# Issuing nine raw parts of w_in from the sync queue, behind the keys and score blocks of chunk 0

## The chip, the cores and the metric

The kernel runs on one core of a Trainium2 chip. The metric is the device time of one execution in microseconds (us). Before the change it is 875.8 us, the median of three runs (874.41 to 876.63). The profiled execution has a span of 874.3 us.

## The reference: delta-rule attention, then a two-layer feed-forward block

There are 4 batches of 8 heads, a sequence of 768 positions and a head size of 48. The attention block keeps a 48 x 48 state per head and walks through the sequence:

```python
k_n = k / (norm(k) + 1e-6)
for t in range(768):
    y[t]  = q[t] @ state
    state = state + beta[t] * outer(k_n[t], v[t] - k_n[t] @ state)
```

Its output, 3072 tokens of 384 numbers, goes through

```python
h = x @ w_in                          # w_in: 384 x 2048
out = (h * sigmoid(1.702 * h)) @ w_out   # w_out: 2048 x 384
```

Both weights reach the kernel as 64-bit floating point, because a 32-bit array is multiplied by a 64-bit scalar where they are made. The kernel has to turn them into 32-bit numbers by itself.

## The kernel before

The sequence is cut into 6 chunks of 128 positions. A unit is one chunk of one batch, so there are 24 units. For every unit the kernel loads keys (KN), queries (QP) and values (V), normalizes the keys, forms score blocks G (keys with keys, keys with queries), writes the key scores to DRAM (Nd) and reads their diagonal 32 x 32 blocks back in another layout (NT). From these, VectorE works out the inverses of triangular blocks (`invert`), and TensorE then solves the units block by block. The feed-forward matmuls (`ph`, `po`) are mixed in between the attention steps as soon as their inputs exist.

For chunk 0 the keys of all four batches are loaded first, and the order is:

```python
    for i in range(B):
        for t, src, dma in ((KN, k, nc.sync.dma_start), (QP, q, nc.scalar.dma_start)):
            if i < len(t):                      # 4 KN tiles, 3 QP tiles at the start
                nc.vector.memset(t[i][:, :, D:DP], 0.0)
                load(i, ((t, src),), dma)
    ...                                         # beta (bI) on the scalar queue
    # -- cut --
    sync = pinned(nc.sync.dma_start)
    for b in range(0, B, HB):
        normalize_first(b)                      # b = 0,1 and then b = 2,3 on VectorE
    ahead(1)                                    # first raw parts of w_in
    run(weights(1, None))                       # convert part 0
    first = [prepare(b) for b in range(B)]
    for b in range(B + 1):
        if b < B:
            next(first[b])                      # transposes of the keys of b
            next(first[b])                      # ... and of the queries
            if b == 0:
                load(len(QP), ((QP, q),), pinned(nc.scalar.dma_start))
            warm(NA0)
        if b > 0:
            run(first[b - 1])                   # scores G of b - 1, then Nd and NT
    run(weights(W0 - 1, None))                  # convert parts 1 and 2
    for b in range(B):
        load_values(b, sync)
    ...
    for i in range(B, len(KN)):
        load(i, ((KN, k), (QP, q)), sync)       # keys and queries of units 4 to 6
    ahead(2)                                    # the next raw parts
    run(invert(0))
    normalize_first(B, len(KN) - B)
    run(weights(W1))
```

`pinned` keeps an instruction behind everything that the program has placed on its engine before. A DMA queue named "sync" is issued by the sync engine (SP in the profile, queue q1), "scalar" by ScalarE (ACT, q10), "gpsimd" by GpSimd (POOL, q0).

The raw weights are fetched in parts. The 12 parts of w_in (three row groups by four column blocks of 512) are staged in the space of w_out. There are six places for them, so parts 6, 7 and 8 take the places of parts 0, 1 and 2. Each fetch consists of four DMAs, for 48 + 16 + 48 + 16 partitions:

```python
    def stage(part):
        if part < parts_in:
            at = part % (2 * KC) * 2 * N_IN     # KC = 3: place part % 6
            return at, at + 2 * N_IN
        ...
    def fetch(part, dma):
        if part < parts_in:
            j, f0 = part % KC, part // KC * N_IN
            parts = list(range(part, part + (KC if part < 2 * KC else 1)))
            ...                                 # 3 parts at once for 0 and 3, else 1
    def convert(part):
        if part in stages:
            dst = target(part)
            from_double(dst, stages.pop(part), dst.shape[-1], part < NA)   # NA = 3
            made.append(part)
            while made and (len(made) > 1 or part >= n_parts - 8):
                taken.pop(made.pop(0), None)    # a place is given free one part later
    def ahead(n, dma=nc.gpsimd.dma_start):
        while n > 0 and waiting and free(waiting[0]):
            staged.extend(fetch(waiting.pop(0), dma))
            n -= 1
    def weights(n, dma=nc.gpsimd.dma_start):
        for _ in range(n):
            if staged:
                convert(staged.pop(staged.index(min(staged))))
            if dma is not None:
                ahead(2, dma)
            yield 0.0
```

`from_double` is six VectorE instructions on 128 x 512 elements for parts 0 to 2 (they are pinned), and five on VectorE and one on ScalarE for the later ones.

Of the kernel before, what the change touches and what calls it, by code (L numbers as in the profile page):

```python
# [18 lines left out]
def kernel(  # L19
# [28 lines left out]
    KC = DM // 128  # L48
# [10 lines left out]
    NA = W0  # L59
# [26 lines left out]
    def load(n, pairs, dma=nc.sync.dma_start):  # L86
        c, b = units[n]
        for dst, src in pairs:
            dma(
                out=dst[n % len(dst)][:, :, 0:D],  # L90
                in_=src[b, :, c * C : (c + 1) * C, :].rearrange("h p d -> p h d"),
            )
# [9 lines left out]
    def pinned(op):  # L102

        return lambda *a, **kw: tc.keep_in_program_order(op(*a, **kw))  # L104
# [45 lines left out]
    def from_double(dst, raw, n, alone):  # L150

        lo, hi = raw[:, :, 0], raw[:, :, 1]
        tmp = wk.tile([128, 2, n], I32, tag="P", name="tmp")
        t0, p = tmp[:, 0], tmp[:, 1]  # L160
        ts, stt = nc.vector.tensor_scalar, nc.vector.scalar_tensor_tensor
        if alone:
            ts, stt = pinned(ts), pinned(stt)
        AND, OR = ALU.bitwise_and, ALU.bitwise_or
        E1 = 1 << 20

        ts(p, hi, 0x7FF * E1, None, op0=AND)
        if alone:
            ts(p, p, -896.0 * E1, 0.0, op0=ALU.add, op1=ALU.max)
            ts(p, p, 255.0 * E1, 8.0, op0=ALU.min, op1=ALU.mult)  # L170
        else:
            nc.scalar.activation(p, p, ACT.Relu, scale=8.0, bias=low)
        ts(t0, hi, E1 - 1, E1, op0=AND, op1=OR)
        stt(out=dst, in0=lo.bitcast(U32), scalar=2.0**-32, in1=t0, op0=ALU.mult, op1=ALU.add)
        stt(out=p, in0=hi, scalar=-(1 << 31), in1=p, op0=AND, op1=OR)
        stt(out=dst, in0=dst, scalar=2.0**-20, in1=p.bitcast(F32), op0=ALU.mult, op1=ALU.mult)  # L176
# [3 lines left out]
    n_parts = parts_in + FC  # L180
# [12 lines left out]
    stages, taken, made = {}, {}, []  # L193

    def stage(part):

        if part < parts_in:
            at = part % (2 * KC) * 2 * N_IN
            return at, at + 2 * N_IN
        f = part - parts_in  # L200
        if f >= FC - 2:
            return None
        depth = 2 if f < 2 or f >= 8 else 4
        if f >= 12:
            depth = 1
        at = FC * DM // (2 if f < 2 else 1) - (f % depth + 1) * 2 * DM
        return at, at + 2 * DM

    def free(part):
        s = stage(part)  # L210
        return s is None or all(s[1] <= a or b <= s[0] for a, b in taken.values())

    def fetch(part, dma):

        if part < parts_in:
            j, f0 = part % KC, part // KC * N_IN
            parts = list(range(part, part + (KC if part < 2 * KC else 1)))
            shape, src = (len(parts), N_IN), moe_w_in[:, f0 : f0 + N_IN]
            dst = w_in[:, j : j + len(parts), f0 : f0 + N_IN]
        else:  # L220
            parts = [part]
            shape, src = (1, DM), moe_w_out
            dst = target(part)
        if src.dtype != F32:
            if (s := stage(part)) is None:
                raw = wk.tile([128, *shape, 2], I32, tag="xT", name="raw", bufs=3)
            else:
                words = slice(s[0], stage(parts[-1])[1])
                raw = w_out.rearrange("p f d -> p (f d)")[:, words].bitcast(I32)
                raw = raw.rearrange("p (j n o) -> p j n o", j=shape[0], o=2)  # L230
            for i, p in enumerate(parts):
                stages[p] = raw[:, i]
                if s is not None:
                    taken[p] = stage(p)
            dst = raw.bitcast(src.dtype).rearrange("p j n o -> p j (n o)")
        if part < parts_in:
            for p, r, m, step in x_rows:
                row = src[r + j * step : r + j * step + m]
                dma(
                    out=dst[p : p + m],  # L240
                    in_=bass.AP(
                        row.tensor, row.offset, [row.ap[0], [row.ap[0][0] * step, len(parts)], row.ap[1]]
                    ),
                )
        else:
            r = (part - parts_in) * 128
            dma(out=dst if src.dtype == F32 else dst[:, 0], in_=src[r : r + 128, :])
        return parts

    def target(part):  # L250
        if part < parts_in:
            j, f0 = part % KC, part // KC * N_IN
            return w_in[:, j, f0 : f0 + N_IN]
        return w_out[:, part - parts_in, :]
# [4 lines that stand above are left out]
            from_double(dst, stages.pop(part), dst.shape[-1], part < NA)  # L259

            made.append(part)
            while made and (len(made) > 1 or part >= n_parts - 8):
                taken.pop(made.pop(0), None)


# [19 lines left out]
    def normalize_first(b0, nb=HB):  # L285

        tt, ts = pinned(nc.vector.tensor_tensor), pinned(nc.vector.tensor_scalar)
        red, recip = pinned(nc.vector.tensor_reduce), pinned(nc.vector.reciprocal)
        stt = pinned(nc.vector.scalar_tensor_tensor)
        mult, add = ALU.mult, ALU.add  # L290
        z = wk.tile([128, 4, nb, H], F32, tag="ksq", name="z", bufs=1)
        sq = wk.tile([128, nb, H, D], F32, tag="G", name="sq", bufs=6)
        x, y, t, s = (z[:, i] for i in range(4))
        for b in range(nb):
            K = KN[(b0 + b) % len(KN)][:, :, 0:D]
            tt(sq[:, b], K, K, op=mult)
            red(s[:, b], sq[:, b], axis=AX.X, op=add)
        ts(x, s, 1e-30, None, op0=ALU.max)
        ts(y.bitcast(I32), x.bitcast(I32), -0.5, float(0x5F3759DF), op0=mult, op1=add)
        for _ in range(3):  # L300
            stt(out=t, in0=y, scalar=-0.5, in1=y, op0=mult, op1=mult)
            tt(t, t, x, op=mult)
            stt(out=y, in0=t, scalar=1.5, in1=y, op0=add, op1=mult)
        tt(s, s, y, op=mult)
        ts(s, s, 1e-6, None, op0=add)
        recip(s, s)
        for b in range(nb):
            K = KN[(b0 + b) % len(KN)][:, :, 0:D]
            tt(K, K, s[:, b].broadcast_to([128, H, D]), op=mult)
# [278 lines left out]
            nc.sync.dma_start(out=out[b * S + c * C : b * S + (c + 1) * C, :], in_=o)  # L588
            yield 1.3

    order = [0, KC] + list(range(2 * KC, n_parts))
    order[-3], order[-2] = order[-2], order[-3]
    waiting, staged = order[:], []

# [13 lines that stand above are left out]
# [11 lines left out]
    def run(work):  # L619
        for _ in work:  # L620
            pass
# [105 lines left out]
    sync = pinned(nc.sync.dma_start)  # L727
    for b in range(0, B, HB):
        normalize_first(b)
    ahead(1)  # L730
    run(weights(1, None))
    first = [prepare(b) for b in range(B)]
    for b in range(B + 1):
# [13 lines left out]
        nc.gpsimd.memset(KN[i][:, :, D:DP], 0.0)  # L747
    for i in range(B, len(KN)):
        load(i, ((KN, k), (QP, q)), sync)
    ahead(2)  # L750
    run(invert(0))
    normalize_first(B, len(KN) - B)
    run(weights(W1))
# [34 lines left out]
```

## Time and profile before

| | |
|---|---|
| Time, median of 3 | 875.8 us |
| Span of the profile | 874.3 us |
| TensorE matmuls busy | 805.2 us (92%) |
| VectorE busy | 488.7 us (56%) |
| ScalarE busy | 209.1 us (24%) |
| GpSimd busy | 115.9 us (13%) |
| DMA queue of the sync engine, q1 | 150528 packets, 40.78 MB |
| DMA queue of GpSimd, q0 | 3328 packets, 12.59 MB |
| DMA queue of ScalarE, q10 | 7168 packets, 1.41 MB |

The busy shares are means over stages that are very different. TensorE is nearly always busy after some 200 us; before that it waits for other engines and partly runs matmuls whose only use is to keep it active (`ps_warm`). In the answers of the trace, a line of the timeline gives the start, the duration, the engine, the line of the kernel, the operation and its tiles, and in brackets how long the engine was idle before it and what ended that. L104 stands for all pinned instructions, because their helper is on that line. The answers on DMA give packets, MB and the time that the packets took as a share of 16 engines; packets [...]overlap, so this share can pass 100%.

### The profile page before, as it was taken

What the parts mean: (1) busy time and instruction counts of PE and PEld (TensorE: products, weight loads), DVE (VectorE), ACT (ScalarE), POOL (GpSimd) and SP (SyncE); (2) the same over time, 40 slices, a digit from 0 to 9 for tenths busy, and PEclk for the clock granted to TensorE, in tenths of its full rate; (3) what the DMA queues carried; (4) which work ended last, traced back from release to release, by engine and by line L of the source; (5) the groups of instructions that cost most, each with busy time, mean ns of one, the idle gap of its engine ahead of it and who ended that gap; (6) DMA issues with size and microseconds to landing.
All of it is one profiled execution on the core that took longest, in us unless ns stands there. A gap on an engine that the chain in (4) does not pass through costs nothing.

```text
span 874.3 us, 15563 instructions
## 1 busy us (share of the span) xinstructions
PE 805.2 (92%) x6564; PEld 595.2 (68%) x6564; DVE 488.7 (56%) x1024; ACT 209.1 (24%) x407; POOL 115.9 (13%) x137
## 2 busy tenths in 40 slices
PE   7601988998999999999999999999999999999998
PEld 5401767865866866867867867867767768677684
DVE  3559968987985394493493592682672760110100
ACT  2300444352322221221312312312312202112020
POOL 3230331231021111101201102102100000000000
PEclk9655999999999999999999999999999999999999
DMA  9695582552223213213213223122132020000000
GB/s 145 118 186 66 124 227 55 137 123 67 47 61 81 49 34 81 49 42 73 57 39 67 59 52 73 38 62 60 25 72 55 3 48 9 1 23 1 14 10 18
DMA packets 161093, 55.76 MB, mean 64 GB/s; under 512 B 128800, under 2 KB 157696, under 8 KB 161024
## 3 DMA queue, kind: packets, MB, share of 16 engines
q1 hardware_dynamic: 150528, 40.78, 22.5%
q0 software_dynamic: 3328, 12.59, 6.3%
q10 hardware_dynamic: 7168, 1.41, 1.2%
q8 instruction: 51, 0.84, 0.4%
q14 instruction: 18, 0.15, 0.1%
HBM read 33.13 MB, written 20.45 MB: 61 GB/s over the span
## 4 chain that ended last, share of the span: by engine, by line
PE 82%; DVE 9%; DMA 6%; issue 1%; ACT 1%; POOL 1%; SPq 0%; DVEq 0%; POOLq 0%
PE po L580 28%; PE ph L565 27%; PE psG L337 5%; PE psY L503 5%; PE psR L478 5%; PE psU L490 4%; PE psT L323 2%; DMA KN<-in_k_dram 2%; PE psR L467 2%; DMA NT<-Nd 2%; PE ps_warm L138 2%; PE psS L522 2%; DVE P L104 1%; DMA Nd<-G 1%; DVE YB L104 1%
## 5 line engine op out<-in xcount | busy, mean ns | idle before, releaser
L565 PE MATMUL ph<-xT,w_in 128*128 128x256 f32 (+1 forms) x1248 | 269.3, 370 | 5.4 <-DMA xT<-last 3.2
L580 PE MATMUL po<-w_out,gT 128*128 128x384 f32 x768 | 268.1, 495 | 3.3 <-DVE w_out L176 3.3
L565 PEld LDWEIGHTS ph<-xT,w_in 128*128 128x128 f32 x1248 | 219.4, 192 | 42.8 <-issue 9.8
L580 PEld LDWEIGHTS po<-w_out,gT 128*128 128x128 f32 x768 | 140.5, 190 | 94.1 <-issue 9.0
L570 ACT ACTIVATE gT<-ph 128x512 f32<-128x512 f32 (+1 forms) x104 | 58.3, 564 | 184.0 <-PE ph L565 183.9
L486 DVE TENSOR_TENSOR V<-V,psR 32x384 f32<-32x384 f32 x92 | 50.6, 550 | 91.7 <-PE psR L478 85.3
L497 ACT COPY U<-psU 32x384 f32<-32x384 f32 x96 | 45.1, 470 | 143.4 <-PE psU L490 93.4
L138 PE MATMUL ps_warm<-ident 128*128 128x256 bf16 x260 | 37.2, 303 | 44.6 <-DVE ps_warm L104 41.5
L478 PEld LDWEIGHTS psR<-U,G 32*32 32x32 f32 (+2 forms) x1152 | 52.7, 107 | 21.9 <-issue 21.3
L478 PE MATMUL psR<-U,G 32*32 32x48 f32 (+2 forms) x1152 | 63.0, 205 | 0.0
L138 PEld LDWEIGHTS <-ident 128*128 128x128 bf16 x260 | 27.3, 108 | 52.1 <-DVE ps_warm L104 42.5
L361 POOL TENSOR_SCALAR_AFFINE_SELECT G<-G 128x1024 f32<-128x1024 f32 x24 | 27.1, 1130 | 257.3 <-DVE G L345 97.7
L337 PE MATMUL psG<-kqT 48*128 48x256 f32 x384 | 58.1, 415 | 1.1 <-ACT kqT L324 0.7
L401 DVE TENSOR_TENSOR P<-NT,YB 64x2 f32<-64x2 f32 (+4 forms) x150 | 52.4, 350 | 4.6
L587 DVE COPY o<-po 128x384 f32<-128x384 f32 x24 | 13.3, 555 | 72.9 <-PE po L580 72.7
L490 PEld LDWEIGHTS psU<-V,XB 32*32 32x32 f32 x1536 | 37.2, 105 | 22.7 <-issue 12.9
L405 DVE TENSOR_REDUCE YB<-P 64x2 f32<-64x2 f32 (+4 forms) x150 | 48.0, 320 | 4.5
L341 ACT ACTIVATE G<-psG 128x512 f32<-128x512 f32 x48 | 28.7, 597 | 75.8 <-PE psG L337 75.6
L490 PE MATMUL psU<-V,XB 32*32 32x48 f32 x1536 | 44.8, 203 | 0.2
L337 PEld LDWEIGHTS psG<-kqT 48*128 48x128 f32 x384 | 35.9, 193 | 10.2 <-issue 2.6
L377 DVE TENSOR_TENSOR NT<-NT,bI 64x1024 f32<-64x1024 f32 x10 | 12.2, 1220 | 50.9 <-DMA NT<-Nd 50.9
L542 DVE COPY last<-psY 48x128 f32<-48x128 f32 x20 | 5.9, 294 | 59.0 <-ACT xT L543 58.1
(81 smaller groups left out, 725.1 us busy)
## 6 DMA issues: line engine op xcount, KB each, us to landing
Nd<-G SPq DMA_DIRECT2D x24, 512.0 KB, 3.2
w_out<-in_moe_w_out_dram POOLq DMA_DIRECT2D x14, 384.0 KB, 4.4
KN<-in_k_dram SPq DMA_DIRECT2D x24, 192.0 KB, 3.4
V<-in_v_dram SPq DMA_DIRECT2D x24, 192.0 KB, 3.3
out_dram<-o SPq DMA_DIRECT2D x24, 192.0 KB, 1.9
QP<-in_q_dram SPq DMA_DIRECT2D x20, 192.0 KB, 2.9
w_out<-in_moe_w_in_dram POOLq DMA_DIRECT2D x16, 192.0 KB, 6.5
NT<-Nd SPq DMA_DIRECT2D x24, 128.0 KB, 2.7
```

Of the source, the lines that this page charges most:

```text
L138: nc.tensor.matmul(ps, lhsT=ones[:, 0:128], rhs=ones, start=True, stop=True)
L337: nc.tensor.matmul(ps[hh][:, i], lhsT=kqT[pr, g + i, 0, :], rhs=kqT[pr, g + i, :, :], start=True, stop=True,)
L401: tt(P, diag(Nf, i * BS, [[0, i], [1, i]]), diag(Yf, 0, [[BS, i], [1, i]]), op=ALU.mult,)
L405: red(diag(Yf, i, [[BS, i]]), P, axis=AX.X, op=ALU.add, negate=True)
L478: nc.tensor.matmul(self.psR[r, h, :], lhsT=self.G[a, h, 0, r], rhs=self.U[a, h, :], start=(self.c == 0 and h == 0), stop=True, skip_group_ ...
L486: nc.vector.tensor_tensor(self.V[r], self.V[r], self.psR[r], op=ALU.subtract)
L490: nc.tensor.matmul(psU[r, h, :], lhsT=self.XB[r, h, :], rhs=self.V[r, h, :], start=True, stop=True,)
L497: nc.scalar.copy(self.U[r], psU[r])
L503: nc.tensor.matmul(self.psY[p : p + D, j, :], lhsT=lhsT(h), rhs=rhs(h), start=start and j == 0, stop=True, skip_group_check=True,)
L565: nc.tensor.matmul(ph[:, u], lhsT=w_in[:, j, f * 128 : (f + 1) * 128], rhs=xT[:, j, t], start=(j == 0), stop=(j == KC - 1),)
L570: nc.scalar.activation(gT[f0 // FQ][:, f0 % FQ : f0 % FQ + 2, t], ph, ACT.Gelu_apprx_sigmoid)
L580: nc.tensor.matmul(po, lhsT=gT[f // FQ][:, f % FQ, i * C : (i + 1) * C], rhs=w_out[:, f, :], start=(f == 0), stop=(f == FC - 1),)
```

## The change

The first two fetches of w_in go to the sync queue. The first (parts 0 to 2) is issued there behind the four key loads of chunk 0. The second call fetches parts 3 to 5 and, in one group instead of three, parts 6 to 8; it stands on the sync queue behind the score blocks, the values and the keys and queries of units 4 to 6. Since parts 6 to 8 now come as one group, the places of parts 0 to 2 have to be given free by their own conversion, which the second hunk does. Parts 9 to 11 and all of w_out remain with GpSimd.

The aim is that the keys, and later the score blocks on their way through DRAM, don't share the DMA engines with weights that are needed later.

```diff
-            parts = list(range(part, part + (KC if part < 2 * KC else 1)))
+            parts = list(range(part, part + (KC if part < 3 * KC else 1)))
...
-            while made and (len(made) > 1 or part >= n_parts - 8):
+            while made and (len(made) > 1 or part < NA or part >= n_parts - 8):
                 taken.pop(made.pop(0), None)
...
-    order = [0, KC] + list(range(2 * KC, n_parts))
+    order = [0, KC, 2 * KC] + list(range(3 * KC, n_parts))
     order[-3], order[-2] = order[-2], order[-3]
...
     for b in range(0, B, HB):
         normalize_first(b)
-    ahead(1)
+    ahead(1, sync)
     run(weights(1, None))
...
     for i in range(B, len(KN)):
         load(i, ((KN, k), (QP, q)), sync)
-    ahead(2)
+    ahead(2, sync)
     run(invert(0))
```

## The prediction

> **What bounds the kernel now.** I read the page first, for where TensorE is not busy (40 slices of 21.9 us):
>
> ```profile
> PE   7601988998999999999999999999999999999998
> DVE  3559968987985394493493592682672760110100
> PEclk9655999999999999999999999999999999999999
> ```
>
> From the tenth slice (about 200 us) TensorE is busy throughout: a fixed amount of matmul work that starts when its inputs exist and ends about 670 us later. So a change to the start pays only if it moves the whole program earlier. TensorE is nearly idle in the third and fourth slices, which the change concerns. Next, the chain of work that ended last (start, us, what), for the first 95 us:
>
> ```profile
> 2.85 20.80 DMA KN<-in_k_dram
> ...
> 42.40 5.22 DMA Nd<-G
> 47.63 10.92 DMA NT<-Nd
> 58.83 1.24 DVE NT L104
> ...
> 84.18 9.75 PE ps_warm L138 x65
> ```
>
> Three transfers of 192, 512 and 128 KB take 20.8, 5.2 and 10.9 us of this chain. The timeline shows the waits that they leave on VectorE (brackets: idle before, and its cause):
>
> ```profile
> 12.81 0.55 DVE L104 TENSOR_REDUCE z<-sq 128x8 f32<-128x384 f32 x1
> ...
> 23.67 0.56 DVE L104 TENSOR_TENSOR sq<-KN 128x384 f32<-128x384 f32 x1 [10.31 <-DMA KN<-in_k_dram]
> ...
> 58.83 1.23 DVE L104 TENSOR_TENSOR NT<-NT,bI 128x1024 f32<-128x1024 f32 x1 [8.34 <-DMA NT<-Nd]
> ```
>
> These are 10.3 and 8.3 us in which VectorE had nothing to do, both ahead of `invert(0)`, which runs 58.83 to 84.06 without a gap. Last, the DMA queues (packets, MB, share) in 8 to 20 us:
>
> ```profile
> q0 software_dynamic: 443, 1.57, 85.6%
> q10 hardware_dynamic: 1118, 0.18, 16.3%
> q1 hardware_dynamic: 546, 0.10, 10.7%
> ```
>
> in 48 to 54 us:
>
> ```profile
> q0 software_dynamic: 254, 0.85, 102.3%
> ```
>
> and in 64 to 72 us:
>
> ```profile
> q1 hardware_dynamic: 7016, 1.33, 150.7%
> ```
>
> The first is the 1.57 MB of parts 0 to 2 (2 x 576 + 2 x 192 KB) while the fourth key tile of 1024 packets of 192 bytes crawls on q1. The second is worse: NT of batch 3 was issued at 47.63, and for 6 us only GpSimd's weights move. The third is q1 alone on small packets: 7016 in 8 us, 877 a us. So the weights, needed later, take the DMA engines while the keys and score blocks, needed now, wait.
>
> [...]q0 alone moves 0.85 MB in 6 us = 141 GB/s. I conclude that the sync queue will not move them faster.
>
> **The change part by part.**
>
> Step 1, keys. Without q0, q1 shares only with q10. By 8 us three key tiles are in. The fourth needs 1024 packets; q1 and q10 together moved 3455 packets in 4 to 8 us (1984 + 1471), so beside what is left on q10 it takes about 2 to 4 us and lands at 11 to 12.5. VectorE is ready for it at 12.81 + 0.59 = 13.40 instead of 23.67: 10.3 us earlier. The second normalization ends at 18.6 instead of 28.9.
>
> Step 2, part 0. The 1.57 MB now start at about 11 on q1 and take 1.57 / 0.131 to 1.57 / 0.141 = 11 to 12 us, so they land at about 22 to 23. Part 0's conversion (3.74 us, 28.80 to 32.54 before) ends at about 26.5. VectorE's first score copy, at 38.87 before, would be due at 28.6, so this new wait of VectorE costs nothing. But beta (bI) and the fourth query tile on q10 share with w_in until 22, and the query tile, which landed at 24.1 (14.59 + 9.5), then comes at about 25.5 to 26. Its transposes were at 35.63 and are due at 25.3: about 0.5 us lost. From here to the last score copy (42.33 before) the shift is about 10 us. TensorE could go faster there: [...]the windows of the trace show 0.60 in 20 to 25 and 0.50 in 25 to 35, after the idle stretch 18 to 28.5 that now goes. Sixteen score matmuls took 2.0 us at 16.0 and 3.8 at 31.0. I count 0 to 2 us for it, as ScalarE's copies limit too.
>
> Step 3, score blocks. The last copy ends at about 32. Nd of batch 3, alone, takes 3.2 us as the second one did (35.94 to 39.15), and NT 2.4 as there: NT is in at about 38. VectorE converts parts 1 and 2 from 32; before they took 42.25 to 50.49, 8.24 us, so it is ready at 40.3. The wait for NT goes, and VectorE is the bound: `invert(0)` starts at about 40.3 instead of 58.83. Gain so far 18.5 us: the two waits of 10.3 and 8.3.
>
> Step 4, the new traffic on the sync queue. Behind NT come 4 V, 3 KN and 3 QP loads, 10240 small packets / 877 = 11.7 us, from 38 to 50. Then parts 3 to 8, 3.15 MB / 0.141 to 0.16 = 20 to 22 us, until about 71. `invert(0)` takes 25.2 us and ends at 65.5, and the results of batches 0 and 2 go out (Yd) and back (XB) on this same sync queue. Before, Yd went at 85.34 and XB followed at 87.77, landing 4.0 later at 91.7, that is 7.7 us after the inversion; TensorE was busy with its 65 warm-up matmuls until 93.93 and used it at once. Now Yd waits behind weights until about 71, and XB is in at about 71 + 2.4 + 4 = 77.5, while TensorE is ready at 65.6 + 9.75 = 75.3. About 2 us back, 4 with slower weights. Part 3, wanted at 67, is in at about 61; part 6, converted about ten us later, comes in time.
>
> Step 5, GpSimd. Of its 32 w_in issues, about 0.5 us each, 20 go (4 + 4 + 3 x 4) and 12 come to the sync queue (3 x 4). GpSimd isn't on the chain in that stage: nothing. The fetches of parts 9 and later depend on the conversions, in the same order, so they move along.
>
> Step 6, to the end. From 85 to 195 us VectorE is busy 4.4 to 5 us in nearly every 5, then TensorE, and all of it follows from the inversion. I let the shift pass whole: 18.5 - 2 = 16.5 us, 875.8 - 16.5 = about 859.
>
> **The rivals.** (a) Yd and XB stuck for longer behind the weights: for it, [...](71 - 65.5) x 0.15 = 0.8 MB of weights may be left when the inversion ends. If V, KN and QP issue as slowly as before (48 to 70 us in the timeline), the weights end near 38 + 22 + 22 = 82, XB comes at 88.5 instead of 75.3, and the gain falls to some 5 us: 871. Against it, those slow issues fell in GpSimd's traffic. (b) Part 0 as the new bound: if w_in lands at 28 rather than 22, VectorE gets to the score copies late and 3 us go: 862. (c) Nothing lost on the way back and the faster TensorE clock counted: invert at 38 and XB hidden behind the warm-up matmuls, 20 us: 855. (d) The gain lost later: the scheduler orders the free instructions anew, and a transfer for chunk 1 (Nd at 115, NT at 120.88, 5.8 and 7.83 us in the chain) doesn't move with the rest; 865. For it: this chain has DMA again at 115 to 129. Against: those issues follow matmuls that shift.
>
> **Range and chances.** The steps give 855 to 862, with (a) and (d) as the tail above: 859, eighty per cent within 852 to 868. Two per cent faster is under 858.3, just under my middle, so 0.44 for that, 0.52 for within two per cent, and 0.04 for slower, which would take a standstill on the sync queue.
>
> **What would show it.** The fourth key tile's wait on VectorE gone and the second normalization at 13.4; `invert(0)` starting near 40 with no wait for NT; q1 carrying w_in at about 140 GB/s from 50 to 71; XB of batch 0 landing some 11 to 12 us after the inversion, and the first solve with it. It is wrong if the inversion starts later than 44, if Yd leaves over 6 us late, or if the first solve is 16 us earlier and the end is not.

## The result and the profile after

The changed kernel takes 864.96 us (median of 4, 862.82 to 866.5), the kernel before beside it on the same chip 875.11 us. The ratio is 0.9885, with a 95% interval of 0.9852 to 0.9917: some 10 us, or 1.15%, faster. The prediction was 859 us with 852 to 868, so the time is 6 us above its middle. The way there is another one than the prediction told.

The page of the changed kernel, 40 slices of 21.6 us:

```profile
PE   8309899989999999999999999999999999999998
DVE  5898569979983592682682772772872851110100
PEclk9759759999999999999999999999999999999999
```

TensorE's empty stretch, two slices wide before (digits 0 and 1), is one slice wide now, though the slice ahead of it is emptier (3 instead of 6). What VectorE did in the first 40 us, by the timeline:

```profile
13.10 0.55 DVE L104 TENSOR_TENSOR sq<-KN 128x384 f32<-128x384 f32 x1
...
23.22 0.78 DVE L104 TENSOR_SCALAR tmp<-w_out 128x512 int32<-128x512 int32 x1 [4.92 <-DMA w_out<-in_moe_w_in_dram]
...
39.48 1.22 DVE L104 TENSOR_TENSOR NT<-NT,bI 128x1024 f32<-128x1024 f32 x1
```

The waits of 10.31 us for the key and of 8.34 us for NT are gone (no brackets), there is a new one of 4.92 us for part 0, and the inversion starts 19.35 us earlier, at 39.48 instead of 58.83. The queues in 48 to 54 us, where GpSimd's weights alone had moved:

```profile
q1 hardware_dynamic: 415, 0.91, 108.9%
```

That is 152 GB/s, now with NT already in. So far it went as planned. The sync engine's part of the timeline then shows the surprise (`XB<-Yd` reads the inverse back that the first solve needs):

```profile
45.65 5.59 SPq L104 DMA_DIRECT2D w_out<-in_moe_w_in_dram  x8
65.97 0.79 SPq L439 DMA_DIRECT2D Yd<-YS  x2
83.23 0.38 SPq L349 DMA_DIRECT2D Nd<-G  x1
83.70 1.95 SPq L444 DMA_DIRECT2D XB<-Yd  x2
```

The same part of the kernel before:

```profile
85.34 0.80 SPq L439 DMA_DIRECT2D Yd<-YS  x2
87.77 1.79 SPq L444 DMA_DIRECT2D XB<-Yd  x2
106.21 0.36 SPq L349 DMA_DIRECT2D Nd<-G  x1
```

In both, Yd leaves as soon as the inversion ends. In the changed kernel XB leaves 17.7 us after it, behind an Nd, the score blocks of unit 4, which belongs to chunk 1. Before, XB followed Yd after 2.4 us and the first Nd of chunk 1 came at 106. What held the sync engine of the changed kernel, by its waits in 30 to 100 us (total, times, longest):

```profile
SPq L349 <- ACT G L343: 16.4, 1, 16.4
```

It stood in front of that Nd for 16.4 us, until ScalarE had copied the scores. TensorE before:

```profile
84.18 9.75 PE L138 MATMUL ps_warm<-ident 128*128 128x256 bf16 x65 [41.52 <-DVE ps_warm L104]
93.86 0.86 PE L490 MATMUL psU<-V,XB 32*32 32x48 f32 x16
```

and in the changed kernel:

```profile
64.80 11.23 PE L138 MATMUL ps_warm<-ident 128*128 128x256 bf16 x83 [32.98 <-DVE ps_warm L104]
...
78.52 1.14 PE L337 MATMUL psG<-kqT 48*128 48x256 f32 x8 [0.96 <-ACT kqT L324]
79.59 0.83 PE L138 MATMUL ps_warm<-ident 128*128 128x256 bf16 x6
80.88 1.61 PE L337 MATMUL psG<-kqT 48*128 48x256 f32 x8 [0.47 <-ACT G L341]
82.43 2.79 PE L138 MATMUL ps_warm<-ident 128*128 128x256 bf16 x24
...
86.83 1.14 PE L337 MATMUL psG<-kqT 48*128 48x256 f32 x8
...
88.66 1.60 PE L337 MATMUL psG<-kqT 48*128 48x256 f32 x8
90.20 2.79 PE L138 MATMUL ps_warm<-ident 128*128 128x256 bf16 x24
...
93.79 0.86 PE L490 MATMUL psU<-V,XB 32*32 32x48 f32 x16
```

After the warm-up matmuls it forms the scores of units 4 and 5 and runs more warm-up matmuls; the first solve (`psU<-V,XB`) comes at 93.79, where it was at 93.86. No brackets stand on it: in the order that TensorE was given it wasn't due sooner. XB had landed at about 88.0, 4.3 us after its issue, so TensorE's own order added the last 6 us. These instructions aren't pinned, so the scheduler of the framework places them, and in the changed program it placed unit 4's and 5's work ahead of the first solve, Nd ahead of XB, and on ScalarE the score copies ahead of the other half of Yd (88.05 instead of 85.34). Why it chose so is not shown; that it expected XB late, behind the weights, is my reading.

Where the 19.35 us went, with the stages cut at four marks (first output: the first `o<-po` copy):

| us | before | after | difference |
|---|---|---|---|
| start to inversion | 58.83 | 39.48 | -19.35 |
| inversion to first solve | 35.03 | 54.31 | +19.28 |
| first solve to first output | 118.29 | 107.38 | -10.91 |
| first output to end of span | 662.2 | 662.6 | +0.4 |

The whole gain is gone at the first solve. Some 11 us come back after it. I put this down to the scores of two units, and what follows from them, being done already, and the runs below agree: from first solve to first output it takes 107.9 us in second_fetch_only, which has the same order, 114.7 in scores_held_back, where one unit's scores stand ahead, and 118.3 and 118.9 in the kernel before and in six_parts_sync, where none do.

### The profile page after: what moved, and what is told of

Read it like the earlier page. It is cut to its first block, busy times and chain, and to the rows that moved or that the text cites. A ratio compares the mean times of both kernels' runs of the same rounds, so it can differ in the third digit from the quotient of the medians.

```text
span 863.8 us, 15545 instructions
## 1 busy us (share of the span) xinstructions
PE 813.2 (94%) x6564; PEld 601.8 (70%) x6564; DVE 489.7 (57%) x1024; ACT 208.6 (24%) x407; POOL 104.8 (12%) x117
## 4 chain that ended last, share of the span: by engine, by line
PE 87%; DVE 7%; DMA 3%; issue 1%; ACT 1%; POOL 1%; ACTq 0%; DVEq 0%; POOLq 0%
PE ph L565 30%; PE po L580 28%; PE psG L337 6%; PE psR L478 5%; PE psY L503 5%; PE psU L490 4%; PE psR L467 2%; PE psT L323 2%; PE psS L522 2%; PE ps_warm L138 2%; DVE P L104 1%; DMA QP<-in_q_dram 1%; DVE YB L104 1%; DMA w_out<-in_moe_w_out_dram 1%; DVE tmp L104 1%
## 5 line engine op out<-in xcount | busy, mean ns | idle before, releaser
L570 ACT ACTIVATE gT<-ph 128x512 f32<-128x512 f32 (+1 forms) x104 | 58.7, 564 | 186.9 <-PE ph L565 186.8
L478 PEld LDWEIGHTS psR<-U,G 32*32 32x32 f32 (+2 forms) x1152 | 56.7, 112 | 23.7 <-issue 21.3
L478 PE MATMUL psR<-U,G 32*32 32x48 f32 (+2 forms) x1152 | 67.3, 212 | 0.5 <-ACT U L497 0.5
L337 PE MATMUL psG<-kqT 48*128 48x256 f32 x384 | 62.2, 420 | 3.9 <-ACT kqT L324 2.8
L490 PEld LDWEIGHTS psU<-V,XB 32*32 32x32 f32 x1536 | 39.6, 109 | 25.2 <-issue 12.2
L490 PE MATMUL psU<-V,XB 32*32 32x48 f32 x1536 | 47.6, 208 | 1.3 <-DVE V L486 1.3
```

The costliest lines, as they stand in the source:

```text
L337: nc.tensor.matmul(ps[hh][:, i], lhsT=kqT[pr, g + i, 0, :], rhs=kqT[pr, g + i, :, :], start=True, stop=True,)
L478: nc.tensor.matmul(self.psR[r, h, :], lhsT=self.G[a, h, 0, r], rhs=self.U[a, h, :], start=(self.c == 0 and h == 0), stop=True, skip_group_ ...
L490: nc.tensor.matmul(psU[r, h, :], lhsT=self.XB[r, h, :], rhs=self.V[r, h, :], start=True, stop=True,)
L570: nc.scalar.activation(gT[f0 // FQ][:, f0 % FQ : f0 % FQ + 2, t], ph, ACT.Gelu_apprx_sigmoid)
```

## The experiments

Each run below computes the whole reference. The expectations name theories by letters. The main two are S, that the order in which the engines issue ate the gain, and R, that Yd and XB are slow on the chip because they share a queue with the weights. Each ratio is against the kernel before as it was timed beside that run (875.11 to 876.64 us). Columns: inversion start, first solve (the first `psU<-V,XB`), the second group of them, first output.

| kernel | median us | ratio (95% interval) | inversion | first solve | second | first output |
|---|---|---|---|---|---|---|
| before | 875.1 | | 58.83 | 93.86 | 100.67 | 212.15 |
| changed | 864.96 | 0.9885 (0.9852-0.9917) | 39.48 | 93.79 | 99.03 | 201.17 |
| first_fetch_only | 867.61 | 0.9900 (0.9884-0.9916) | 47.96 | 82.42 | 89.23 | 202.43 |
| second_fetch_only | 875.31 | 0.9994 (0.9983-1.0005) | 49.67 | 103.92 | 108.72 | 211.81 |
| gpsimd_held | 879.83 | 1.0043 (1.0029-1.0057) | 45.85 | 84.56 | 96.69 | 220.29 |
| yd_on_scalar | 866.77 | 0.9878 (0.9843-0.9913) | 41.52 | 75.46 | 90.42 | 200.70 |
| six_parts_sync | 859.11 | 0.9804 (0.9785-0.9823) | 38.78 | 75.23 | 82.90 | 194.13 |
| six_and_scalar | 860.24 | 0.9826 (0.9780-0.9871) | 40.46 | 75.73 | 85.04 | 195.78 |
| six_more_warm | 872.89 | 0.9955 (0.9936-0.9973) | 41.63 | 78.56 | 89.72 | 200.15 |
| scores_held_back | 870.23 | 0.9947 (0.9927-0.9968) | 40.69 | 90.40 | 94.07 | 205.12 |
| nine_program_order | 864.71 | 0.9870 (0.9845-0.9896) | 39.38 | 74.07 | 97.23 | 202.01 |
| before_program_order | 875.76 | 1.0008 (0.9993-1.0022) | 57.78 | 92.94 | 104.34 | 210.59 |
| six_program_order | 858.07 | 0.9801 (0.9770-0.9831) | 41.09 | 75.78 | 86.13 | 192.84 |
| nine_all_order | 857.11 | 0.9779 (0.9747-0.9812) | 40.57 | 75.09 | 87.28 | 193.72 |

**The two fetches apart: first_fetch_only and second_fetch_only.** Each puts one of the two calls back to GpSimd:

```diff
-    ahead(2, sync)        # first_fetch_only
+    ahead(2)
```

> Only parts 0 to 2 on the sync queue, parts 3 to 8 from GpSimd at once. The key wait (10.3 us) goes, the NT wait comes back as GpSimd's weights run beside Nd and NT. Inversion at about 47 to 50, first solve about 9.8 us after its end (order as before): 82 to 85; all theories 864 to 868 us. If the end moves by as much as the inversion, P falls.

```diff
-    ahead(1, sync)        # second_fetch_only
+    ahead(1)
```

> Only parts 3 to 8 on the sync queue, parts 0 to 2 from GpSimd. The key wait stays, the NT wait (8.3 us) goes: inversion at about 50.5. The instruction order is the one of the changed kernel, with the scores of units 4 and 5 ahead of the first solve. S: about 9 us of the gain go to that order, so 873 to 877 us, no gain or nearly none. Without S the 8.3 us would come through: 866 to 868.

With the first fetch alone the inversion starts 10.9 us earlier, the first solve 11.4 and the first output 9.7: the shift passes to the end, and the time (0.990) is nearly that of the whole change. The wait left on VectorE is another than expected: none for NT, but a longer one for part 0.

```profile
30.78 0.43 DVE L104 TENSOR_SCALAR tmp<-w_out 128x512 int32<-128x512 int32 x1 [12.25 <-DMA w_out<-in_moe_w_in_dram]
```

It was 4.92 us in the changed kernel; here parts 3 to 5 are left to GpSimd. So the forecast inversion time came true for another reason. With the second alone the inversion starts 9.2 us earlier, and nothing of it arrives. The sync engine's timeline of second_fetch_only:

```profile
76.15 0.80 SPq L439 DMA_DIRECT2D Yd<-YS  x2
93.36 0.38 SPq L349 DMA_DIRECT2D Nd<-G  x1
93.82 1.95 SPq L444 DMA_DIRECT2D XB<-Yd  x2
```

It is the same picture as in the changed kernel: Nd ahead of XB, XB 17.7 us after Yd. In the kernel with the first fetch alone XB follows Yd after 2.4 us. So the second fetch brings the new order with it, and in the changed kernel it gains about as much as it costs.

**The weights held back on GpSimd's queue: gpsimd_held.** All nine parts stay with GpSimd, in the same groups, and a tiny copy into the staging places holds each fetch until a late key or query tile has come.

```diff
+    def hold(part, tile_):
+        at = stage(part)[0]
+        nc.gpsimd.tensor_copy(w_out.rearrange("p f d -> p (f d)")[:, at : at + 1], tile_[:, 0, 0:1])
...
-    ahead(1, sync)
+    hold(0, KN[B - 1])
+    ahead(1)
...
-    ahead(2, sync)
+    for p in (0, KC):
+        hold(p, QP[(len(KN) - 1) % len(QP)])
+    ahead(2)
```

> The same nine parts in the same groups, but issued by GpSimd as before and held back by tiny copies into their staging places: the first fetch until the fourth key tile of chunk 0 has landed, the second until the last query load of unit 6 has landed. The sync queue carries no weights. If the early gain comes from when the weights move and not from which queue moves them, VectorE's waits for keys and NT go here too and the inversion starts at 39 to 42; with the instruction order of before and Yd not behind weights, S expects the first solve at 75 to 78 and 856 to 860 us. If it is the queue itself[...], the inversion starts at 45 or later and 865 us or more.

By the marks set beforehand (inversion at 45 or later, 865 us or more) this falls on the side of the queue itself. But the first hold let go only at 18.6, after the key's normalization, later than meant; the part 0 wait grew to 7.55 us and the inversion starts at 45.85. So the run doesn't separate the two for the time. It does for the waits: those for the key and for NT are gone here too, so it is the time of the weights, not the kind of queue, that removes them. The order is the one of the kernel before, although the groups are those of the change, so the grouping alone doesn't bring the new order. The first solve is 9.3 us earlier than before; still the end is later. The second state update, at 146.7 before, is at 141.0, and the third at 189.9 instead of 180.0. What delays it there I didn't settle; GpSimd's later issues moved as well.

The run also shows what weights on another queue do to Yd. Yd was issued at 72.27; the queues in 72 to 78 us:

```profile
q0 software_dynamic: 242, 0.85, 105.9%
```

No packet of q1 or q10 is among them; in 78 to 84 these two move 2702. XB could be issued 9.0 us after Yd. On the sync queue behind the weights this distance is 5.0 (nine_all_order, six_parts_sync), with no weights about 2.4 (before). R is therefore real, but small: 2.6 us.

**Yd and XB off the sync queue: yd_on_scalar.**

```diff
-            eng = nc.scalar if c == 0 and b % 2 == 1 else nc.sync
+            eng = nc.scalar if c == 0 else nc.sync
```

> Change as it is, but all four pairs Yd and XB of chunk 0 go on ScalarE's queue; nothing else. Theory S (order): the weights on the sync queue make the scheduler expect XB late, so it puts the scores of units 4 and 5 ahead of the first solve and Nd ahead of XB; here it puts the first solve first again, so the 19.35 us won at the inversion come through: first solve at 75 to 77 (93.8 in the changed kernel), 855 to 858 us. Rival R (queue on chip): the weights hold the DMA engines until 70.7 whoever issues Yd, XB lands at 78 or later. Rival P (not passed on): later stages absorb it whatever the first solve does, 863 to 866 us.

The order is again that of the kernel before, the first solve comes at 75.46 as S said, but the end, 866.77, misses S's 855 to 858 and lies by P's 863 to 866 (P: later stages absorb whatever the first solve gains; six_parts_sync and nine_all_order below refute it). The sync engine's waits in 30 to 100 us show why:

```profile
SPq L104 <- DMA Yd<-YS: 20.8, 2, 18.1
```

The last three weight DMAs wait for the Yd of another queue, the first of them for 18.1 us and 20.8 us in all, and leave only at 70.00 to 73.77. VectorE pays:

```profile
81.50 0.43 DVE L167 TENSOR_SCALAR tmp<-w_out 128x512 int32<-128x512 int32 x1 [3.84 <-DMA w_out<-in_moe_w_in_dram]
...
86.58 0.55 DVE L486 TENSOR_TENSOR V<-V,psR 32x384 f32<-32x384 f32 x1
```

The subtraction that the second solves need is behind ten conversion instructions, and these solves come at 90.42. Why DMAs without data in common wait for each other is not shown.

**Less on the sync queue: six_parts_sync, six_and_scalar, six_more_warm.** The first is the changed kernel with parts 6 to 8 back on GpSimd, but in one group:

```diff
-    ahead(2, sync)
+    ahead(1, sync)
```

> Change as it is, but parts 6 to 8 are left to GpSimd as one group, so only six parts go on the sync queue and they end there at about 60 instead of 70.7, before the inversion ends at 64.7. Yd and XB stay on their queues. S: the scheduler sees a short queue and keeps the first solve in front; first solve at 75 to 77, 855 to 859 us. R: the same or slightly better than with Yd on ScalarE's queue, as nothing is left on the DMA engines. P: 863 to 866.

859.11 us, ratio 0.9804: faster than the changed kernel, the intervals apart. Its sync engine and its TensorE:

```profile
56.13 2.56 SPq L104 DMA_DIRECT2D w_out<-in_moe_w_in_dram  x4
65.27 0.79 SPq L439 DMA_DIRECT2D Yd<-YS  x2
70.27 1.80 SPq L444 DMA_DIRECT2D XB<-Yd  x2
83.94 0.36 SPq L349 DMA_DIRECT2D Nd<-G  x1
```

```profile
64.11 11.19 PE L138 MATMUL ps_warm<-ident 128*128 128x256 bf16 x80 [32.98 <-DVE ps_warm L104]
75.23 0.86 PE L490 MATMUL psU<-V,XB 32*32 32x48 f32 x16
```

XB is ahead of Nd, and the first solve follows the warm-ups. Yet the sync queue was not free sooner on the chip, as had been expected: parts 3 to 5 left only at 56.13 to 58.7, and q1 still moved 0.67 MB in 64 to 68 us, when it was to be empty from 60 on. Yd waits behind weights here as in the changed kernel and is back 5.0 us later; that the first solve comes 18.6 us earlier all the same speaks against R. From the first solve to the first output it takes 118.9 us, as before the change (118.3): the 18.6 us at the first solve are 18.0 at the output.

six_and_scalar adds the edit of yd_on_scalar to it:

> Six parts on the sync queue (parts 6 to 8 from GpSimd) and all Yd and XB of chunk 0 on ScalarE's queue. With Yd on ScalarE's queue alone the last three weight DMAs on the sync queue waited 18.1 us for a Yd to land, and VectorE then 3.8 us for weights; with six parts no weight DMA is left behind Yd. S: first solve at 75, as with six parts alone, 857 to 861 us: no better than six parts, as the queue is empty by then. If ScalarE's queue itself was the reason for the poor result, 864 to 868.

860.24, no different from six_parts_sync, though the reason given ("the queue is empty by then") doesn't hold: the weights leave only at 57.40 to 59.8, over a microsecond later than in six_parts_sync, and Yd leaves at 66.95, when the DMA engines move 170 GB/s (65 to 70). six_more_warm adds warm-up matmuls in the steps after the first solve, because TensorE's granted clock is 0.64, 0.50 and 0.84 in the three windows of 5 us from 105 to 120 in six_parts_sync:

```diff
-    NW, NA0, NY, NB0 = 80, 3, 48, 6
+    NW, NA0, NY, NB0 = 80, 3, 48, 10
```

> Six parts on the sync queue, and ten instead of six warm-up matmuls at each place where the feed-forward queue is empty (NB0). Six parts alone show TensorE's clock at half from 105 to 120. If that half clock costs time on the way to the end, 853 to 857 us; if TensorE only waits there for other engines (it waited 5.7 us for xT just then), 858 to 862 us, or slower by the matmuls added.

A clear miss: 872.89, some 14 us slower than without. The second solves fall back from 82.90 to 89.72, of which 3.3 us are there at the first solve already, and the first output comes 6.0 us later. The half clock wasn't what to cure: these matmuls stand between the steps of a chain of dependent solves, at 1.3 us for every 10. Where the rest of the 14 us arises, after the first output, wasn't traced.

**The order undone, in steps: scores_held_back, nine_program_order, nine_all_order.** These three keep all nine parts on the sync queue. The first pins only the transposes, the kqT copies and Nd of units 4 and 5:

```diff
-                nc.tensor.transpose(psT[:, j, :], flat[:, j * 128 : (j + 1) * 128], ident)
+                turn(psT[:, j, :], flat[:, j * 128 : (j + 1) * 128], ident)
...
+        store = pinned(nc.sync.dma_start) if B <= n < B + 2 else nc.sync.dma_start
```

> Change as it is, all nine parts on the sync queue, but the transposes of units 4 and 5, the copies of their results and their Nd are kept behind what stands ahead of them in the program. That puts Nd behind XB on the sync queue and takes unit 5 and part of unit 4's wait out of the way; 156 warm-up matmuls and unit 4's scores still stand ahead of the first solve on TensorE (65 and nothing before). S, counting 0.12 us a warm-up matmul and 3 us for unit 4: first solve at 84 to 87, between 93.8 and 75, and 858 to 864 us. R: first solve at 77 to 79, as the weights end at 70.7.

XB is issued at 72.15, so one cause is gone, but the first solve comes at 90.40, later than either theory said, and the time, 870.23, is outside S's 858 to 864 and some 5 us above the changed kernel's:

```profile
77.97 3.33 PE L138 MATMUL ps_warm<-ident 128*128 128x256 bf16 x29
82.56 1.14 PE L339 MATMUL psG<-kqT 48*128 48x256 f32 x8 [1.26 <-ACT kqT L104]
...
85.93 4.54 PE L138 MATMUL ps_warm<-ident 128*128 128x256 bf16 x40
90.40 0.86 PE L493 MATMUL psU<-V,XB 32*32 32x48 f32 x16
```

TensorE still has unit 4's scores and 72 warm-ups ahead of it, after 83 warm-ups in front of those, and only one unit's scores are done in exchange. nine_program_order therefore holds every matmul of TensorE, the kqT copies and Nd of the first steps in the order of the program text:

```diff
+    strict = [False]
+    def mm(*a, **kw):
+        op = nc.tensor.matmul
+        return (pinned(op) if strict[0] else op)(*a, **kw)
...
-            nc.tensor.matmul(                  # and so for all matmuls, kqT and Nd
+            mm(
...
+        strict[0] = n < 2
```

> Change as it is: all nine parts on the sync queue, Yd and XB where the change has them. Only the instruction order is fixed: for the first slots TensorE's matmuls and transposes, the copies of the transposes and Nd keep program order, so 66 warm-up matmuls and no scores of units 4 and 5 stand ahead of the first solve, Nd behind XB, and Yd on ScalarE's queue ahead of the score copies. S: the first solve comes as soon as XB has landed behind the weights (end 70.7), at 76 to 79, about 15 us earlier than in the changed kernel, and the end is 856 to 861 us. R (XB late because of the queue on the chip): first solve at 88 or later and 863 to 867 us.

The first solve comes at 74.07, with the weights still on the queue to about 70.7: R falls for the first batch. The end, 864.71, misses S's 856 to 861 and is that of the changed kernel all the same. ScalarE and TensorE:

```profile
79.54 0.82 ACTq L444 DMA_DIRECT2D Yd<-YS  x2
```

```profile
74.07 0.86 PE L104 MATMUL psU<-V,XB 32*32 32x48 f32 x16
...
86.92 1.48 PE L104 MATMUL psR<-U,G 32*32 32x48 f32 x16 [8.39 <-ACT U L502]
...
97.23 0.87 PE L104 MATMUL psU<-V,XB 32*32 32x48 f32 x32
```

The other half of Yd stands on ScalarE behind conversions of w_in and leaves 13.6 us after its data is ready; behind it stands XB, and behind XB the copy of U that TensorE awaits for 8.39 us. nine_all_order holds these too:

```diff
-            nc.scalar.activation(p, p, ACT.Relu, scale=8.0, bias=low)
+            (pinned(nc.scalar.activation) if strict[0] else nc.scalar.activation)(p, p, ACT.Relu, scale=8.0, bias=low)
...
-            eng.dma_start(out=XB, in_=Yd.rearrange("(h t) i -> t h i", h=H))
+            reads.append((eng, XB, Yd))
+        for eng, XB, Yd in reads:
+            go = pinned(eng.dma_start) if c == 0 else eng.dma_start
+            go(out=XB, in_=Yd.rearrange("(h t) i -> t h i", h=H))
...
+    strict[0] = True                       # from the conversions on, not only the slots
     run(weights(W1))
...
-            nc.scalar.copy(self.U[r], psU[r])
+            (pinned(nc.scalar.copy) if strict[0] else nc.scalar.copy)(self.U[r], psU[r])
```

> All nine parts stay on the sync queue as in the changed kernel. In nine_program_order TensorE's instructions, the kqT copies and Nd of the first slots were held in program order; here ScalarE's conversions of w_in and the copies of U are held too, and the loads Yd of chunk 0 are all issued ahead of the XBs. S (what cost the gain is the order in which the engines issue, not the queue on the chip): ScalarE's Yd leaves at 66 instead of 79.5, XB lands at 75 to 79 behind the weights (end about 70.7), the first solve is at 74 to 79, the second group of solves at 84 to 90 instead of 97.2, the end at 857 to 862. R (the queue itself delays): ScalarE's Yd and XB, issued at 66, land after 80 all the same, the second group of solves is at 93 or later, and the end stays at 863 to 867.

S's numbers hold, with Yd leaving at 67.07 for 66: 857.11 us, ratio 0.9779. ScalarE's loads and TensorE's solves:

```profile
67.07 0.85 ACTq L445 DMA_DIRECT2D Yd<-YS  x2
72.37 1.26 ACTq L104 DMA_DIRECT2D XB<-Yd  x2
```

```profile
75.09 0.84 PE L104 MATMUL psU<-V,XB 32*32 32x48 f32 x16 [0.42 <-DMA XB<-Yd]
...
79.46 0.86 PE L104 MATMUL psR<-U,G 32*32 32x48 f32 x16
...
87.28 0.87 PE L104 MATMUL psU<-V,XB 32*32 32x48 f32 x32
```

Against the kernel before, the inversion is 18.3 us earlier, the first solve 18.8, the first output 18.4, and the span 18.6 (855.7). The queue, the bytes and the groups are those of the changed kernel; only the order on the engines differs. The order thus cost the changed kernel some 8 us, less whatever the further pins may be worth by themselves.

**Control and combination: before_program_order, six_program_order.** The pinning of nine_program_order could be worth something by itself, so the kernel before was given it:

> Control: the kernel before with the same fixing of the instruction order and nothing of the change. The order there was already first solve first, so the inversion stays at 58.8, the first solve at 93 to 95 and the time at 872 to 878 us; a gain here would mean that the fixing itself helps and not the order that the change lost.

It isn't: 1.0008. The further pins of nine_all_order have no such control. Six parts with that pinning:

> Six parts on the sync queue, parts 6 to 8 from GpSimd, and the instruction order fixed as in the run with nine parts. First solve at 74 to 76 in both theories; 855 to 860 us, the same as six parts without fixing or a little better than nine parts with it, as no weights stand ahead of Yd.

858.07, ratio 0.9801. six_parts_sync, six_program_order and nine_all_order have overlapping intervals, so I don't rank them; all three are faster than both kernels of this case, by about 2% against the one before. six_parts_sync differs from the change by one number.

## Why the prediction was right, and where it was not

The time lies in the range, but one step failed, and it is in part luck that the middle is so near.

**Step 1 (keys): right.** Second pair at 13.10 instead of the predicted 13.40, no wait left.

**Step 2 (part 0): right.** It landed at 23.2 for 22 to 23, and the wait of 4.92 us cost nothing later: the last score copy ended at 31.5 (about 32 predicted). The query tile came at 24.2, sooner than the 25.5 to 26 feared.

**Step 3 (score blocks): right.** The inversion starts at 39.48 for about 40.3; 19.35 us gained for 18.5. VectorE was the bound, as said.

**Step 4 (the traffic on the sync queue): the step that failed.** Its data on the chip were right: q1 at 152 GB/s for the estimated 141 to 160 (a little faster than q0's 141, against the conclusion drawn from that), the weights through at about 71 as predicted, Yd issued at 65.97. Its conclusion, "XB is in at about 71 + 2.4 + 4 = 77.5", held the issue order of before for granted. XB was issued at 83.70, 19.0 us after the inversion's end, and the first solve came at 93.79, so "about 2 us back" was 19.3 us. With the order held (nine_all_order) the first solve takes XB at 75.09 and the step's term is right again. Rival (a), a long queue, would have looked much the same at the first solve; the trace speaks against it, since XB wasn't issued until 83.70, some 12 us after Yd had landed (5.4 us after its issue). Rival (d) named the cause, that "the scheduler orders the free instructions anew", but put it at transfers of chunk 1 and gave it the tail. Its 865 was the measured time, by another way.

**Step 5 (GpSimd): right.** Its busy time fell from 115.9 to 104.8 us, 0.55 for each of 20 issues, and nothing shows for it.

**Step 6 ("I let the shift pass whole"): right as to the rule.** From the first output to the end of the span it is 662.2 us before, 662.6 after, 662.0 in nine_all_order. Between first solve and first output the changed kernel is 10.9 us quicker, which the step didn't foresee; the work done ahead of the first solve is saved there. So the error of step 4 was 17 us and about two thirds of it were given back: 859 + 17 - 11 = 865. That the middle was missed by only 6 us is luck: two effects that the prediction didn't have cancelled in great part.

Of the signs given for being right, the last failed: XB did not land 11 to 12 us after the inversion with the first solve behind it. The sign given for being wrong, a first solve 16 us earlier with the end unmoved, didn't occur in the changed kernel. Something near it occurs in yd_on_scalar and nine_program_order, whose first solves are over 18 us earlier than before and whose ends only some 10: one batch's solve was not the mark to watch there, the group behind it was.

## What to carry to other kernels

When a transfer moves to another queue, instructions that aren't pinned may come out in another order, as they did here: after such a change, compare the order of issue on every engine ahead of the first dependent step before blaming the queue. If the order is the cause, pin the whole ring of engines that pass data round; here a part of it pinned gave nothing (nine_program_order) or lost some 5 us (scores_held_back). And when two things are moved in one change, run each alone: here one of them carried nearly the whole gain.

## What the runs showed of the hardware that was not expected

With weights on q0, nothing of the other queues moved for 6 us in two runs; behind weights on its own queue Yd only took 2.6 us longer. In 48 to 54 us of the kernel before and 72 to 78 us of gpsimd_held only q0 moved, 0.85 MB each, with NT or Yd issued and waiting, and Yd to XB took 9.0 us beside weights on q0 against 5.0 behind weights on q1 and about 2.4 without weights. It is no rule: in 56 to 60 us of the kernel before both queues moved, 1923 records of q1 and 177 of q0. The standstill of the kernel before goes on to 55 us, with 339 records of q0 from 48 on; what ends it stays open.

TensorE's granted clock differed where its busy time did not. The windows of 5 us (PE busy, ..., granted clock, DMA share, GB/s), of the changed kernel and of nine_all_order:

```profile
105.00:110.00 5.00, 3.34 (x71) 2.77 (x67) 3.65 (x7) 0.94 (x2) 0.53 (x1) 0.50 0.00 0
```

```profile
105.00:110.00 5.00, 4.22 (x68) 3.47 (x68) 4.49 (x7) 2.64 (x5) 1.59 (x3) 1.00 0.99 308
```

The changed kernel runs at half clock from 100 to 125, nine_all_order at full, with TensorE busy for 22.1 and 21.3 of the 25 us. The fall came between 96 and 97 us (0.61 granted). In the three microseconds before it TensorE was busy for 1.00, 0.66 and 0.25, with no gap above 1.10 us, while nine_all_order kept 1.00 in 120 to 125 us, busy for 2.97 of the 5. What the fall followed stays open. Nor is full clock worth any price: in 105 to 115 us six_more_warm has 1.00 where six_parts_sync has 0.64 and 0.50, and it is slower.
